# Describing the source of a contiguous load as 32 long rows while the destination keeps 128

## The chip, the cores and the metric

The kernel runs on one core of a Trainium2 chip. The metric is the device time of one launch in microseconds, the median of several executions. Besides the times there is one profiled execution, and all durations of single steps come from it.

## What is computed

The reference applies two layers to one token of width 640. Each layer is a sliding-window attention over a cache, followed by a mixer with an MLP, and both layers use the same weights and the same cache:

```python
x = x + _A_ref(_layernorm(x, axis=-1), A_k_cache, A_v_cache, A_wq, A_wo)
x = x + _B_ref(_layernorm(x, axis=-1), B_w1, B_w2, B_w3, B_w4)
x = x + _A_ref(_layernorm(x, axis=-1), A_k_cache, A_v_cache, A_wq, A_wo)
x = x + _B_ref(_layernorm(x, axis=-1), B_w1, B_w2, B_w3, B_w4)

def _A_ref(x, k_cache, v_cache, wq, wo):       # Hq = Hkv = 32, Dh = 192, Sk = 32768, D = 640
    W = min(4096, max(256, Sk // 4))           # 4096
    q = (x @ wq).reshape(B, Sq, Hq, Dh).transpose(0, 2, 1, 3)
    k = k_cache[:, :, Sk - W:, :]
    v = v_cache[:, :, Sk - W:, :]
    p = softmax(einsum("bhqd,bhkd->bhqk", q, k) * Dh ** -0.5)
    o = einsum("bhqk,bhkd->bhqd", p, v)
    return o.transpose(0, 2, 1, 3).reshape(B, Sq, Hq * Dh) @ wo

def _B_ref(x, w1, w2, w3, w4):                 # D = 640, F = 1536
    h = gelu(layernorm(x) @ w1)
    g0..g3 = quarters of h, shifted by one or two positions along S and padded with zeros
    x1 = x + concatenate([g0, g1, g2, g3]) @ w2
    return x1 + gelu(layernorm(x1) @ w3) @ w4
```

All tensors are bf16. As the sequence has one position, the shifted quarters are all zero, so w1 and w2 never matter and the kernel does not load them. Per layer and head it needs the last 4096 positions of K and V, 1.5 MiB each.

## The kernel before

One load of K or of V brings one head's window, 4096 x 192 values, into a buffer called a cell: 128 partitions with 6144 values (12,288 B) each, where partition p holds 32 consecutive positions. The source is contiguous through all partitions: the row of partition p + 1 starts in memory where that of p ends. There are twelve cells (`take` and `give` hand them out and take them back), shared by K, V, the transposed copies of K, the pieces of wo and the mixer's weights.

All loads are issued by SP on one queue, in the order of `stream`: wq in five pieces (`load_wq`, L178, one contiguous 128 x 6144 block each) with the input x after the first, then layer 0 and layer 1 by `layer_stream`. Within a layer the heads come in eight groups of four; a head's K load (`load_k`, L149) runs about a group ahead of its V load (`load_v`, L154), and after a group comes the piece of wo (`load_wo`, L182, 128 rows of 7,680 B, contiguous too) that its four heads need. A layer ends with w3 and w4 (`load_w3`, `load_w4`), whose rows are 2,560 and 3,072 B long. A few V loads are split into parts, each of which takes some columns of every row, and so do two pieces of wo at the end of layer 1. Layer 1 does not load K for heads 0 to 7 (`NKEEP`), since their transposed copies are kept, nor V of heads 2 and 3, and only a part of V for head 4.

SP issues a load as soon as its cell is free and the queue takes it. Per head, DVE transposes K in 32 x 32 blocks (L398), PE forms the scores (L474), the softmax follows for four heads at once (L494 to L561), PE multiplies with V (L590), DVE transposes the result (L597), and the group's output goes through wo. At the end of a layer the mixer (L881) multiplies with w3 (L922) and w4 (L969).

```python
    def load_k(layer, h):
        t = take(("k", layer, h))
        nc.sync.dma_start(t[:], A_k_cache[0, h, s0:Sk, :].rearrange("(p j) d -> p (j d)", p=P))
        return t
```

Of the kernel before, what the change touches and what calls it, by code (L numbers as in the profile page):

```python
# [2 lines left out]

# [14 lines left out]
P = 128  # L18
# [13 lines left out]
NJ4, NGK, NM = 4, 8, 4  # L32

RING = 1024


def shrink_ring(nc):


    nc.dynamic_dma_scratch_size = RING  # L40
    for a in nc.allocations:
        for m in getattr(a, "memorylocations", ()):
            if m.name == "DynamicDMAScratchLoc":
                m.dims = [P, RING]


@with_exitstack
def kernel(
# [13 lines left out]
):  # L62
    nc = tc.nc
    shrink_ring(nc)
    _, _, D = A_x.shape
    _, H, Sk, Dh = A_k_cache.shape
# [18 lines left out]
    s0 = Sk - W  # L85

    NA = Dh // 32
    NKX, NKL = 6, 8
    NKEEP, NCELL = 8, 12
# [11 lines left out]

    above, nc.sbuf_base = (nc.sbuf_base + 31) // 32 * 32, RING
    low = ctx.enter_context(tc.tile_pool(name="low", bufs=1))
# [18 lines left out]
        name=nc.get_next_instruction_name(), act_func_set_id=ACT_TABLE_SET, ins=[], outs=[]))  # L122

    wq_sb = fixed.tile([P, ND, HD], BF16, name="wq_sb")
# [10 lines left out]
    def take(key):  # L135
        i = free.popleft()
        cell_of[key] = i
        return (low if i == NCELL - 1 else cells).tile([P, FREE], BF16, tag=f"cell{i}", name=f"cell{i}")

    def give(key):  # L140
        free.append(cell_of.pop(key))

    def load_x():

        x_bf = wx_sb[0:ND, 4 * P:5 * P]
        nc.sync.dma_start(x_bf, A_x.rearrange("a b (n p) -> (a b n) p", p=P))
        return x_bf

    def load_k(layer, h):  # L149
        t = take(("k", layer, h))  # L150
        nc.sync.dma_start(t[:], A_k_cache[0, h, s0:Sk, :].rearrange("(p j) d -> p (j d)", p=P))
        return t

    def load_v(layer, h):  # L154
        t = take(("v", layer, h))
        src = A_v_cache[0, h, s0:Sk, :].rearrange("(p j) d -> p (j d)", p=P)
        cut = (2 * VW,) if h == VP else (FREE - VN, FREE - NKX * Dh) if h == VX else ()
        if h in GROUPS[layer][-1][-1 - layer:]:
            cut = FREE // 2,
        i = 0  # L160
        for e in cut + (FREE,):
            kept_v = h == VP or h == VX and i > 0
            if layer == 0 or not kept_v:
                nc.sync.dma_start(v_pair(t, h, i, e - i), src[:, i:e])
            i = e
        return t

    def v_pair(V, h, i, n):

        if h == VP and i >= 2 * VW:  # L170
            V, i = loaded["wo", 0, 0], i - 2 * VW + NA * D
        elif h == VX and i >= FREE - NKX * Dh:
            V, i = kx, i - (FREE - NKX * Dh)
        elif h == VX and i >= FREE - VN:
            V, i = kl, i - (FREE - VN)
        return V[:, i:i + n]

    def load_wq(layer, kc):  # L178
        nc.sync.dma_start(wq_sb[:, kc, :], A_wq[kc * P:(kc + 1) * P, :])
        return wq_sb  # L180

    def load_wo(layer, c):  # L182
        t = take(("wo", layer, c))
        src = A_wo[c * QC:(c + 1) * QC, :].rearrange("(p c) n -> p (c n)", c=NA)
        parts = {NG - 2: (3, 3), NG - 1: (3, 2, 1)}.get(c, (NA,)) if layer == 1 else (NA,)
        i = 0
        for n in parts:
            nc.sync.dma_start(t[:, i * D:(i + n) * D], src[:, i * D:(i + n) * D])
            i += n
        return t  # L190
# [13 lines left out]
    def load_w4(layer):  # L204
# [17 lines left out]
        return blocks  # L222

    LOADERS = {"x": load_x, "k": load_k, "v": load_v, "wq": load_wq, "wo": load_wo, "w3": load_w3, "w4": load_w4}

    def layer_stream(layer):
# [797 lines left out]
```

## Time and profile before

| | us |
|---|---|
| median of 3 runs | 515.57 (515.52 to 516.28) |
| the profiled execution, its own time | 515.88 |
| its span | 514.1 |
| PE busy | 325.7 (63%) |
| DVE busy | 291.2 (57%) |
| ACT busy | 48.9 (10%) |
| K load, 1536 KB, issue to landing (median) | 26.3 |
| V load, 1536 KB, issue to landing (median) | 27.3 |
| wo load, 960 KB, issue to landing (median) | 25.3 |

The span runs from the first to the last recorded instruction; the execution's own time has 1.8 us more around it. The granted TensorE clock was 0.669 on average. The loads read 214.5 MB. The line of slices cuts the span into 40 parts of 12.9 us, each digit a busy share in tenths; under it stands the rate at which data moved. In the view by windows the columns after the stretch are its length, the busy time of each engine with its instructions, the granted clock, the share of the 16 DMA engines' time that packets took, and the rate. In the chain of waits a line is start, length, and what the end of the program hung on then. Issue lines show the time at which SP handed a load over and how long the handing over took.

### The profile page before, as it was taken

The page shows a single profiled execution, that of the slowest core. Times are in us where ns is not written, and L with a number is a line of the kernel's source. Part 1 is how long each engine was busy: PE and PEld are TensorE (multiplying, and loading weights), DVE is VectorE, ACT ScalarE, POOL GpSimd, SP SyncE. Part 2 cuts the span into 40 slices and gives each one's busy share as a digit, 9 for nine tenths or more (in the row PEclk, how much of TensorE's full clock was granted, in tenths as well). Part 3 has the DMA queues.
Part 4 walks back from the last instruction along what each step waited for, and adds up shares of the span by engine and source line. Part 5 has one row for each costly group of instructions (what it writes and reads, how often), then busy time and mean ns, then how long its engine had stood idle before and what let it go on. Part 6 is the DMA issues. An engine that isn't in the chain of part 4 may idle for free.

```text
span 514.1 us, 9455 instructions
## 1 busy us (share of the span) xinstructions
PE 325.7 (63%) x4084; PEld 190.2 (37%) x4084; DVE 291.2 (57%) x587; ACT 48.9 (10%) x173; POOL 4.0 (1%) x16
## 2 busy tenths in 40 slices
PE   1057658656576645857655767667676766767665
PEld 0023334333333323534333544434343443335335
DVE  2077656676565755467623244666576566756722
ACT  1000101010010100101011111001010100100011
POOL 2000000000000000000000000000000000000000
PEclk9995777777665776576675585675565577656765
DMA  8999999999999999999999899999999999999996
GB/s 348 432 429 428 429 428 429 427 428 428 429 431 428 429 424 430 432 423 430 427 420 415 344 409 430 429 425 428 427 431 427 429 427 431 427 428 431 429 413 251
DMA packets 24093, 215.11 MB, mean 418 GB/s; under 512 B 2548, under 2 KB 3060, under 8 KB 9076
## 3 DMA queue, kind: packets, MB, share of 16 engines
q1 hardware_dynamic: 24052, 214.51, 99.0%
q8 instruction: 32, 0.52, 0.4%
q14 instruction: 9, 0.07, 0.0%
HBM read 214.50 MB, written 0.00 MB: 417 GB/s over the span
## 4 chain that ended last, share of the span: by engine, by line
DMA 54%; PE 23%; DVE 18%; issue 3%; ACT 1%; SPq 1%; DVEq 0%; ACTq 0%
DMA cell<-in_A_k_cache_dram 26%; DMA cell<-in_A_v_cache_dram 20%; DVE cell L398 13%; PE ST_ps L474 10%; PE O_ps L590 7%; DMA cell<-in_B_w_dram 4%; DMA cell<-in_A_wo_dram 4%; DVE o_sb L597 2%; PE qT_ps L428 1%; PE l_ps L549 1%; PE PT_ps L544 1%; PE nb_ps L522 1%; DVE pm L499 1%; DVE o_sb L533 1%; DVE V_ps L579 1%
## 5 line engine op out<-in xcount | busy, mean ns | idle before, releaser
L474 PE MATMUL ST_ps<-cell,Qblk 128*16 128x256 bf16 x1536 | 159.4, 375 | 104.9 <-DVE cell L398 68.4
L398 DVE STREAM_TRANSPOSE cell<-cell 128x768 uint32<-128x768 uint32 x224 | 200.4, 944 | 12.1 <-DMA cell<-in_A_k_cache_dram 11.8
L474 PEld LDWEIGHTS <-Qblk 128*16 128x16 bf16 x1536 | 83.7, 110 | 173.6 <-issue 147.5
L590 PE MATMUL O_ps<-cell,PT 128*2 128x384 bf16 x1010 | 101.3, 473 | 7.7 <-DMA cell<-in_A_v_cache_dram 5.6
L597 DVE STREAM_TRANSPOSE o_sb<-O_ps 128x384 f32<-128x384 f32 x64 | 37.2, 581 | 112.7 <-PE O_ps L590 112.6
L590 PEld LDWEIGHTS <-PT 128*2 128x2 bf16 x1024 | 46.2, 102 | 23.1 <-issue 14.6
L533 DVE STREAM_TRANSPOSE o_sb<-o_sb 128x256 bf16<-128x256 bf16 x16 | 7.1, 445 | 33.8 <-ACT o_sb L528 25.0
L605 ACT ACTIVATE oT<-oT_ps,rl 32x6 bf16<-32x6 f32 x40 | 10.3, 257 | 158.4 <-PE oT_ps L604 149.7
L604 PE MATMUL oT_ps<-o_sb,Lq 128*32 128x6 f32 x160 | 13.9, 195 | 11.1 <-DVE o_sb L597 10.6
L604 PEld LDWEIGHTS oT_ps<-o_sb,Lq 128*32 128x32 f32 x160 | 12.8, 144 | 21.6 <-issue 15.9
L610 ACT ACTIVATE oT<-oT_ps,rl 32x6 bf16<-32x6 f32 x24 | 6.2, 257 | 111.0 <-PE ST_ps L474 95.8
L428 PE MATMUL qT_ps<-xc,wq_sb 128*128 128x1 bf16 x210 | 7.2, 165 | 13.0 <-DMA wq_sb<-in_A_wq_dram 12.1
L417 PE MATMUL qr_ps<-wq_sb,xc 128*1 128x384 bf16 x90 | 14.1, 468 | 0.0
L442 DVE TENSOR_TENSOR Xq<-qT_ps,maskq 128x24 bf16<-128x24 f32 (+1 forms) x18 | 2.9, 162 | 18.2 <-PE qT_ps L428 17.5
L544 PE MATMUL PT_ps<-o_sb,Eq 128*32 128x32 bf16 x256 | 7.2, 237 | 9.2 <-DVE o_sb L533 4.0
L636 PE MATMUL yr_ps<-cell,oT 128*1 128x320 bf16 x108 | 12.3, 380 | 0.0
L428 PEld LDWEIGHTS <-wq_sb 128*128 128x128 bf16 x210 | 6.8, 104 | 14.2 <-DMA wq_sb<-in_A_wq_dram 13.2
L525 ACT COPY nb_sb<-nb_ps 128x1 f32<-128x1 f32 x16 | 2.6, 160 | 94.4 <-PE nb_ps L522 94.4
L549 PE MATMUL l_ps<-lh,ones 128*128 128x4 f32 x32 | 8.4, 334 | 4.9 <-ACT PT L547 4.9
L544 PEld LDWEIGHTS <-Eq 128*32 128x32 bf16 x256 | 5.5, 111 | 16.0 <-issue 15.9
L609 PE MATMUL oT_ps<-o,Lq 128*32 128x6 f32 x48 | 6.1, 200 | 6.0 <-DVE o L608 6.0
L522 PEld LDWEIGHTS nb_ps<-ones,o_sb 1*128 1x128 f32 x32 | 7.1, 275 | 7.2 <-issue 5.4
(146 smaller groups left out, 196.8 us busy)
## 6 DMA issues: line engine op xcount, KB each, us to landing
cell<-in_A_k_cache_dram SPq DMA_DIRECT2D x56, 1536.0 KB, 26.3
cell<-in_A_v_cache_dram SPq DMA_DIRECT2D x56, 1536.0 KB, 27.3
cell<-in_A_wo_dram SPq DMA_DIRECT2D x13, 960.0 KB, 25.3
wq_sb<-in_A_wq_dram SPq DMA_DIRECT2D x5, 1536.0 KB, 12.2
cell<-in_A_v_cache_dram SPq DMA_DIRECT2D x6, 768.0 KB, 23.3
cell<-in_A_v_cache_dram SPq DMA_DIRECT2D x2, 864.0 KB, 9.0
cell<-in_B_w_dram SPq DMA_DIRECT2D x1, 1536.0 KB, 12.0
cell<-in_B_w_dram SPq DMA_DIRECT2D x2, 768.0 KB, 10.3
```

Source lines behind the costliest of these rows:

```text
L398: nc.vector.transpose(Tu, Ku[:, :, q * NY:(q + 1) * NY])
L417: nc.tensor.matmul(qr_ps[32 * i:32 * i + 1, :], lhsT=xc[:, kc:kc + 1], rhs=wq_sb[:, kc, t0 * P + i * N:t0 * P + (i + 1) * N], start=(kc == ...
L428: nc.tensor.matmul(qT_ps[:, tl:tl + 1], lhsT=wq_sb[:, kc, t * P:(t + 1) * P], rhs=xc[:, kc:kc + 1], start=(kc == 0), stop=(kc == ND - 1))
L474: nc.tensor.matmul(ST_ps[r:r + QW, :].rearrange("p (g i) -> p g i", g=ng), lhsT=Q[:, n, :], rhs=T4[:, :, f, :, t], start=(hq == 0 and n == ...
L522: nc.tensor.matmul(nb_ps[:], lhsT=held["w"], rhs=ones[0:1, 0:1], start=True, stop=True)
L533: nc.vector.transpose(held["PrT"], held["Pr"])
L544: nc.tensor.matmul(PT_ps[32 * m:32 * (m + 1), :, :, ng * q:ng * (q + 1)], lhsT=Eq[:, q, :], rhs=src[:, m:QW:NM], start=True, stop=True)
L549: nc.tensor.matmul(l_ps[:], lhsT=ones[:], rhs=held["lh"][:], start=True, stop=True)
L590: nc.tensor.matmul(O_ps[r:r + 2, :], lhsT=PT[:, hq, 2 * i:2 * i + 2], rhs=v_pair(V, h, 2 * i * Dh, 2 * Dh), start=(i < 4), stop=(i >= NB - 4))
L597: nc.vector.transpose(o_sb[:], O_ps.rearrange("p (e a c) -> p e c a", e=2, c=NA))
L604: nc.tensor.matmul(oT_ps[r, :], lhsT=Lq[:], rhs=o_sb[:, e, :, e], start=(e == 0), stop=(e == 1))
L636: nc.tensor.matmul(yr_ps[32 * i:32 * i + 1, :], lhsT=oT[:, k:k + 1], rhs=wo_t[:, k * D + i * N:k * D + (i + 1) * N], start=(k == 0), stop= ...
```

## The change

A helper `load_wide` issues a load whose source is described as 32 rows, each four times as long, and whose destination is described as before. The instruction is put together by hand, since the two sides have different shapes; both name the same bytes in the same order, and it goes to the same queue on SP. `load` chooses between it and `dma_start`. All K loads use it except the first K load of layer 1; all V loads that aren't split, except heads 0 and 1 in layer 1; wq except its first piece; wo where it is not split. The order of the loads and all other instructions stay.

```diff
+WIDE = 4
...
+def load_wide(nc, dst, src):
+    wide = src.rearrange("(g w) n -> g (w n)", w=WIDE)
+    assert [list(d) for d in wide.ap] == [[WIDE * src.shape[1], P // WIDE], [1, WIDE * src.shape[1]]]
+    sym = [mybir.BassSymbolicTensorAccessPattern(ap=a.ap, dtype=a.dtype, bass_ap=a) for a in (wide, dst)]
+    return nc.sync.add_instruction(mybir.InstDMACopy(
+        name=nc.get_next_instruction_name(), ins=sym[:1], outs=sym[1:], queue="qSPDynamicHW", mode="Copy"))
...
+    def load(dst, src, wide=True):
+        (partial(load_wide, nc) if wide else nc.sync.dma_start)(dst, src)
...
     def load_k(layer, h):
         t = take(("k", layer, h))
-        nc.sync.dma_start(t[:], A_k_cache[0, h, s0:Sk, :].rearrange("(p j) d -> p (j d)", p=P))
+        load(t[:], A_k_cache[0, h, s0:Sk, :].rearrange("(p j) d -> p (j d)", p=P), (layer, h) != (1, NKEEP))
...
     def load_v(layer, h):
...
-            if layer == 0 or not kept_v:
+            if not cut:
+                load(t[:], src, layer == 0 or h >= 2)
+            elif layer == 0 or not kept_v:
                 nc.sync.dma_start(v_pair(t, h, i, e - i), src[:, i:e])
...
     def load_wq(layer, kc):
-        nc.sync.dma_start(wq_sb[:, kc, :], A_wq[kc * P:(kc + 1) * P, :])
+        load(wq_sb[:, kc, :], A_wq[kc * P:(kc + 1) * P, :], kc > 0)
...
     def load_wo(layer, c):
...
+        if len(parts) == 1:
+            load(t[:, 0:NA * D], src)
+            return t
         for n in parts:
             nc.sync.dma_start(t[:, i * D:(i + n) * D], src[:, i * D:(i + n) * D])
```

More of the change, by code (lines that the diff above doesn't have):

```diff
@@ L2 @@
 from contextlib import ExitStack
+from functools import partial
 import concourse.bass as bass
```

## The prediction

> **What bounds the kernel now.** I read the page's slices first, because they say whether any engine is busy all the time. None of the compute engines is; the DMA engines are.
>
> ```profile
> span 514.1 us, 9455 instructions
> PE 325.7 (63%) x4084; PEld 190.2 (37%) x4084; DVE 291.2 (57%) x587; ACT 48.9 (10%) x173; POOL 4.0 (1%) x16
> ...
> DMA  8999999999999999999999899999999999999996
> GB/s 348 432 429 428 429 428 429 427 428 428 429 431 428 429 424 430 432 423 430 427 420 415 344 409 430 429 425 428 427 431 427 429 427 431 427 428 431 429 413 251
> DMA packets 24093, 215.11 MB, mean 418 GB/s; under 512 B 2548, under 2 KB 3060, under 8 KB 9076
> ...
> q1 hardware_dynamic: 24052, 214.51, 99.0%
> ```
>
> PE works 63% of the span and DVE 57%, while the DMA engines stand at nine tenths or more in nearly all 40 slices, at 423 to 432 GB/s in the steady ones. The loads' queue, q1, fills 99.0% of 16 engines' time. The only visible hole is the slice of 344 GB/s, near 289 us, where the first layer's mixer hands over to the second layer's attention.
>
> Next the stretches, from the view by windows, and the queue's issues in order of time:
>
> ```profile
> core 0: us, PE busy (x) PEld busy (x) DVE busy (x) ACT busy (x) POOL busy (x), PEclk, DMA share, GB/s
> 108.26:139.84 31.58, 19.93 (x219) 11.06 (x218) 19.75 (x37) 3.04 (x10) 0.00 (x0) 0.72 1.01 428
> ...
> 340.00:380.00 40.00, 29.13 (x314) 15.57 (x309) 25.00 (x47) 5.28 (x17) 0.00 (x0) 0.56 1.01 428
> ...
> 276.00:284.00 8.00, 5.25 (x118) 4.17 (x110) 2.11 (x16) 1.64 (x8) 0.00 (x0) 0.50 1.00 397
> ...
> 288.00:292.00 4.00, 3.48 (x76) 2.35 (x79) 0.90 (x6) 0.30 (x2) 0.00 (x0) 0.50 0.81 308
> ...
> 111.96 0.33 SPq L164 DMA_DIRECT2D cell<-in_A_v_cache_dram  x1
> 115.61 0.33 SPq L151 DMA_DIRECT2D cell<-in_A_k_cache_dram  x1
> 119.25 0.33 SPq L164 DMA_DIRECT2D cell<-in_A_v_cache_dram  x1
> ```
>
> A DMA share of 1.01 means that no engine rests and that neighbouring packets overlap a little. SP hands over a load every 3.65 us, and its own issue takes 0.33 us. A group of four heads (eight K or V loads and one wo load) repeats every 31.58 us. Where rows are shorter (276 to 284 us, the mixer's weights, rows of 2,560 and 3,072 B) the same full share moves only 397 GB/s: rows cost something beyond their bytes.
>
> Last the chain of waits, to see whether the compute side would keep up if the loads came faster:
>
> ```profile
> 76.72 27.84 DMA cell<-in_A_k_cache_dram
> ...
> 108.26 27.84 DMA cell<-in_A_k_cache_dram
> ...
> 423.61 28.41 DMA cell<-in_A_v_cache_dram
> 452.09 28.39 DMA cell<-in_A_v_cache_dram
> ...
> 499.91 10.49 DMA cell<-in_B_w_dram
> ```
>
> The chain is nearly all DMA up to 200 us and again from 423.6 to 510.4 us. A load takes about 28 us from issue to landing: 7.6 loads of 3.65 us stand in line, so what a load waits for is its turn. From 285 to 423 us the chain runs through PE and DVE steps. It is the time in which compute, left behind at the layers' border, catches up, while the queue stays full.
>
> **What one row costs.** The trace records each packet: rows of 12,288 B take 460 ns (median of 14,976), 7,680 B 291, 3,072 B 121, 1,280 B 55, and the 4 B that report a landing 9 ns. From 55 to 460 ns that is (460 − 55)/(12,288 − 1,280) = 0.03679 ns per byte, and 460 − 452.1 = 7.9 ns per row that no byte explains; 291 and 121 ns fit the same line. But packets overlap, so the wall pays less. One engine moves (8 × 1,572,864 + 983,040)/16 = 847,872 B in a group; at 0.03679 ns per byte this is 31.19 us of the 31.58. The remaining 386 ns are spread over 72 rows and 9 reports: 4.8 ns each. So 7.9 ns is the upper price of a row on the wall, 4.8 ns what the queue in motion shows.
>
> **The change, part by part.** It removes no byte and no load, and it leaves the order on every engine alone. What it changes is the source side of 126 loads: 55 of K, 54 of V, 4 of wq, 13 of wo. Each reads 32 rows of 49,152 B (30,720 B for wo) instead of 128; the destination keeps its 128 rows. Per engine a wide load reads 2 rows, not 8, so 126 × 6 = 756 source rows per engine go away. Left as they were: the first wq load, the second layer's first K load and first two V loads, all split loads, the mixer's weights.
>
> The cost of a source row by itself is not shown: in all rows of this trace source and destination have equal lengths. It is bounded by 0 (the destination's rows carry the whole cost) and 7.9 ns; below 0 is possible if unequal sides lose the overlap (a rival below). I take 4.8 ns, all of it on the source side, since that is what the full queue shows in the very stretches where the wide loads lie. 756 × 4.8 ns = 3.6 us. By 7.9 ns it would be 6.0 us, by 0 nothing.
>
> [...]
>
> All of the saving lies on the path, as the wide loads lie in stretches with a share of 1.01. In the hole about 1.4 us of DMA time is lost because cells are not free (shares of 0.81, 0.92 and 0.96 in three windows of 4 us from 288 us on, against 1.01); it starts from the landing of the first layer's w4, comes earlier with it, and stays. The tail from 510.4 us stays as well. Between 285 and 423 us compute covers its lag: its groups there take 29.6 and 30.3 us (same DVE step at 349.38, 379.02 and 409.31 us) against the queue's 31.58. With a group of loads at 31.58 − 54 × 0.0048 = 31.32 us it still gains 1.0 to 1.7 us per group, where it gained 1.3 to 1.9. The lag it made up by 423 us, in 4.5 groups, is some 7 us; at the new rate that takes about five groups, to 445 us, well before the loads end. If that cover were gone, the second layer's share of the gain (53 of the 126 loads, 1.5 us) would go with it.
>
> SP's instruction has sides of unequal shape now. Its price isn't in the trace. Nearest rows: 0.33 us for an even load, 0.38 to 0.50 us for the mixer's three-dimensional ones. Anything below 3.65 us is hidden behind the queue in motion; at the start, four wq loads take 2.19 us to issue, and a rise to 0.5 us each adds nothing, as the queue has a load to move by then. I price it at 0, with up to 0.5 us if the start shows it.
>
> Sum: the profiled execution took 515.88 us (span 514.1, 1.8 around it), 0.31 over the median of 515.57. 515.88 − 3.6 = 512.3 on its own scale, and 512.0 on the median's. A kernel of this spread can tell 0.2%, 1.0 us, from no change.
>
> **The rivals.**
>
> Destination rows set the pace. Each engine still writes 128/16 = 8 rows of 12,288 B per load, and if the 4.8 ns belong to writing, or the generator cuts the long row to the shorter side, nothing moves: 515.6. For it: the price of a row is known only with both sides together. Against it: nothing in the trace. 0.12.
>
> The memory sets the pace, whatever the rows. Then too 515.6. Against it speaks the window of 397 GB/s with short rows at full share beside 428 with long ones. [...] 0.02.
>
> Slower: unequal sides lose the overlap. Today each packet overlaps the next by 7.9 − 4.8 = 3.1 ns. If with one read feeding four writes every destination row pays its full 7.9 ns, 126 × 8 = 1,008 rows per engine pay 3.1 ns more: +3.1 us, 518.7. A pause between long reads decides: there are 252 per engine, so the 3.6 us are used up at 14 ns per long read, and beyond that the kernel is slower. For it: no row in the trace has unequal sides, so a pause of that size is not excluded. Against it: the report of 4 B between rows costs only 9 ns. 0.18.
>
> A part of the gain: both sides share the cost, or the start of layer two gives some back. 513 to 514.5, counted with faster.
>
> [...]
>
> **How the numbers follow.** The forecast with its spread, from a part of the gain to 7.9 ns per row (509.6 to 514.5), has 0.68; no change 0.14; slower 0.18. The range runs from 509.3, the upper price, to 516.2, which takes in no change and its scatter; outside it lie most of the slower case and a few hundredths below. The likeliest case alone spans 509.6 to 514.5.
>
> **What would show it.** Right: q1 falls from 24,052 packets by up to 126 × 96 = 12,096, the steady slices rise from 428 to 431 or 433 GB/s, a group repeats in 31.3 us, the first layer's w4 lands near 283 instead of 285.1 us, and the hole keeps its depth. Wrong in size: the count falls and the slices stay at 428 (destination rows pay). Wrong in sign: the slices fall below 427, or the share of the steady windows drops under 1.00, which would be pauses between long reads. If the slices rise but the end does not come earlier, the chain from 285 us on must show compute to the end.

## The result: 0.23% faster, a third of the forecast

The changed kernel's median is 514.79 us and that of the kernel before 515.86 us, 17 runs of each in turns; the ratio is 0.9977, 95% interval 0.9969 to 0.9986, that is 1.2 us less (0.7 to 1.6). The forecast was 3.6 us less. The profiled execution took 513.87 us with a span of 512.1. It is the quickest of the 17, while the profiled execution of the kernel before, 515.88 us, lies at its median; so the 2.0 us between the two traces' spans flatter the change.

The page of the changed kernel:

```profile
span 512.1 us, 9455 instructions
...
DMA  8999999999999999999999999999999999999996
GB/s 369 430 430 427 432 439 430 439 427 415 454 433 427 434 408 425 430 416 451 428 403 417 351 444 427 424 436 420 434 427 420 430 439 427 424 439 430 419 407 240
DMA packets 11997, 215.11 MB, mean 420 GB/s; under 512 B 2548, under 2 KB 3060, under 8 KB 7412
...
q1 hardware_dynamic: 11956, 214.51, 98.4%
```

q1 has exactly the 12,096 packets fewer that the long rows allow: the trace has 3,616 packets of 49,152 B, 1,820 ns each in the median, where a packet of 12,288 B took 460. The queue's packet time sank from 99.0% of 514.1 us to 98.4% of 512.1, by 5 us per engine. The steady slices now jump between 408 and 454 GB/s, because the page books a packet as a whole where it begins and a packet is four times as large; only long windows can be compared. Two of them, the view by windows of the kernel before:

```profile
core 0: us, PE busy (x) PEld busy (x) DVE busy (x) ACT busy (x) POOL busy (x), PEclk, DMA share, GB/s
20.00:260.00 240.00, 151.33 (x1723) 85.78 (x1723) 149.74 (x262) 19.81 (x68) 0.00 (x0) 0.70 1.01 428
310.00:470.00 160.00, 110.02 (x1243) 61.29 (x1235) 102.81 (x181) 15.83 (x54) 0.71 (x2) 0.60 1.01 428
```

and of the changed kernel:

```profile
20.00:260.00 240.00, 152.15 (x1725) 87.12 (x1726) 149.61 (x262) 20.20 (x70) 0.00 (x0) 0.73 1.00 430
310.00:470.00 160.00, 110.14 (x1236) 61.97 (x1236) 102.43 (x181) 15.60 (x53) 0.71 (x2) 0.61 1.00 431
```

The rate rose in both, but the share fell from 1.01 to 1.00. Some 2 of the 5 us reached the wall, as the next sums show; the rest, by the share, was time in which packets had overlapped.

To compare finer than this view, I spread every loading packet's bytes evenly over its own time. From 20 to 260 us the rate, which I call the steady rate, is then 427.2 GB/s before and 429.3 after, +0.5%. From the same sums comes the time at which so many bytes had moved. Against the kernel before, the changed one gains 1.15 us between 10 and 110 MB (the first layer's stream) and 0.84 us between 130 and 210 MB (the second's), 2.0 us together. I call this sum the stream's gain; it leaves out the start, the border of the layers and the end. About 115 of the 126 wide loads lie in those bytes, so it is 17.3 ns per load.

SP's issues, in order of time, show the other difference, 0.47 us each instead of 0.33:

```profile
111.23 0.47 SPq L55 DMA_DIRECT2D cell<-in_A_v_cache_dram  x1
115.05 0.47 SPq L55 DMA_DIRECT2D cell<-in_A_k_cache_dram  x1
118.67 0.47 SPq L55 DMA_DIRECT2D cell<-in_A_v_cache_dram  x1
```

### The profile page after: what moved, and what is told of

Same layout as the page of the kernel before. It is cut to its first block, busy times and chain, and to the rows that moved or that the text cites. A ratio compares the mean times of both kernels' runs of the same rounds, so it can differ in the third digit from the quotient of the medians.

```text
span 512.1 us, 9455 instructions
## 1 busy us (share of the span) xinstructions
PE 326.1 (64%) x4084; PEld 191.4 (37%) x4084; DVE 290.9 (57%) x587; ACT 48.8 (10%) x173; POOL 4.0 (1%) x16
## 3 DMA queue, kind: packets, MB, share of 16 engines
q1 hardware_dynamic: 11956, 214.51, 98.4%
## 5 line engine op out<-in xcount | busy, mean ns | idle before, releaser
L494 PE MATMUL ST_ps<-cell,Qblk 128*16 128x256 bf16 x1536 | 161.3, 378 | 102.7 <-DVE cell L418 67.9
```

Of the source, the lines that this page charges most:

```text
L494: nc.tensor.matmul(ST_ps[r:r + QW, :].rearrange("p (g i) -> p g i", g=ng), lhsT=Q[:, n, :], rhs=T4[:, :, f, :, t], start=(hq == 0 and n == ...
```

## The experiments

**A stream of loads alone.** Two questions: what does a row cost on either side, and does the kernel's other work eat part of the gain? The first kernel holds nothing but loads, described in several ways:

```diff
+        for rs, rd in SEGMENTS:          # rows of the source and of the destination
+            for _ in range(LOADS):
+                load(nc, t[:], src, rs, rd)
```

> Leaves the whole computation out: it only streams K loads of 1.5 MiB into ten buffers, 20 loads per stretch, and writes zeros. Eight stretches, told by source rows / destination rows of a load per DMA engine: 8/8 as before, 2/8 as in the change, 4/8, 16/16, 8/16, 4/16, then 8/8 and 2/8 again. In the profiled runs of the two kernels the steady rate from 20 to 260 us was 427.2 and 429.3 GB/s, that is 7.0 ns per row over the bytes before, and 2.9 ns saved per source row taken away. Theory A (both sides pay: a source row 2.9 ns, a destination row 4.1 ns): 427.4, 429.5, 428.8, 421, 423.6, 425 GB/s in order. Rival B (a source row costs all of the 7.0 ns, but a long read that feeds several destination rows pauses about 12 ns): 427.4, 429.3, 424.8, 421, and 416 or less for 8/16. Rival C (all cost on the source side and no pause; what is missing in the kernel is lost to the kernel's own traffic): 427.4, 432.5, 430.8, 421, 427.4, 431.

Measured from the packets in the middle of each stretch: 8/8 427.2, 2/8 426.4, 4/8 426.3, 16/16 417.6, 8/16 417.8, 4/16 417.8, then 426.3 and 426.4 GB/s. None of the theories said this. Apart from the first stretch, whose 427.2 comes from its first loads (below), the number of source rows means nothing here; only the destination's count does, by (3,765 − 3,689)/8 = 9.5 ns per row. Yet the kernel had gained. A difference between the two was the address: these buffers began 128 B past a multiple of 256 B in their partition, the kernel's cells at multiples of 256. So I streamed again with both.

> Leaves the whole computation out, as the first stream did, with 16 loads per stretch. In that one the buffers began 128 B past a multiple of 256 B in each partition; the kernel's cells begin at multiples of 256. Here six stretches begin at multiples of 256 (source rows / destination rows per load and engine: 8/8, 2/8, 4/8, 16/16, 8/16, 4/16), then 128 B past it 8/8 and 2/8, 64 B past it 8/8, and 128 B past it 8/16. Theory M (an engine reads and writes side by side, and the slower side sets the pace; 8.1 ns per source row, about 5 ns per destination row that begins at a multiple of 256 B, 9 ns for one that does not): 427, 429.5 to 430, the same for 4/8, 420, 426, 426, then 426.3, 426.3, about 426.3, and 417.8 GB/s. Theory S (costs of both sides add up, 2.9 and 1.1 ns in the kernel, and the stream alone differed because no other engine touched the memory): addresses change nothing, so 8/8, 2/8 and 4/8 stand at 426 to 427 and all stretches with 16 destination rows at 417.7.

| source/destination rows per engine and load | destination row begins at a multiple of 256 B plus | GB/s, mean of the stretch | ns per load |
|---|---|---|---|
| 8/8 | 0 | 430.0 | 3,657 |
| 4/8 | 0 | 431.8 | 3,642 |
| 2/8 | 0 | 432.6 | 3,636 |
| 8/16 | 0 | 429.2 | 3,664 |
| 4/16 | 0 | 429.7 | 3,661 |
| 16/16 | 0 | 425.7 | 3,695 |
| 8/8 | 128 | 426.4 | 3,688 |
| 2/8 | 128 | 426.4 | 3,689 |
| 8/8 | 64 | 426.2 | 3,690 |
| 8/16 | 128 | 417.8 | 3,765 |

The view by windows of this stream shows the stretches with 12,288-byte packets (8/8 and 8/16 on a multiple of 256 B, and in the other order of addresses 8/8 and 8/16 at 128 B past):

```profile
core 0: us, DVE busy (x) POOL busy (x), PEclk, DMA share, GB/s
10.00:53.00 43.00, 0.00 (x0) 0.00 (x0) 1.00 1.01 430
245.00:287.00 42.00, 0.00 (x0) 0.00 (x0) 1.00 1.01 429
362.00:405.00 43.00, 0.00 (x0) 0.00 (x0) 1.00 1.01 427
539.00:583.00 44.00, 0.00 (x0) 0.00 (x0) 1.00 1.01 417
```

With the source held at 8 rows, twice the destination rows cost 0.8 GB/s in the first pair and 8.6 in the second, by the table. On multiples of 256 B the two sides seem to add up: a source row costs (3,657 − 3,636)/6 = 3.6 ns, and from 8/16 to 16/16 it is 3.8; a destination row costs 0.9 ns beside 8 source rows. 128 B past them, eight more destination rows cost 77 ns (3,688 and 3,765), 9.6 ns each, and the source's rows nothing (3,688 with 8, 3,689 with 2). Theory M expected the role of the address, but by its prices it said 420 for 16/16; theory S had the sums and missed the address. So I took theory A2 into the next runs: costs add up while destination rows are aligned; otherwise the destination's rows alone set the pace.

Two things speak against adding up. In the table four source rows are worth 3 ns from 8/16 to 4/16, not 14; and the first stream's first stretch was faster than its repeat. Taken load by load, from the same packets, the stretches show why:

| stretch | ns of its loads, in order |
|---|---|
| 8/8 on a multiple of 256 B | after the first load, 3,657 or 3,658 each to the end |
| 2/8 on a multiple of 256 B | six of 3,629 or 3,630, one of 3,633, then 3,640 each to the end |
| 8/16 on a multiple of 256 B | 3,658 or 3,659 for most of the first eight (one 3,698), 3,662, then 3,665 or 3,666 |
| 8/8 at 128 B past, first in its stream | after the first load four of 3,657 or 3,658, 3,675, then 3,688 to 3,690 |

The last three begin at a pace that goes by their source rows (3,658 ns for 8 rows, whatever the destination; 3,630 for 2) and settle at a slower one. 4/16, which follows 8/16, has no fast loads at its start (3,661 ns in the mean). What goes on inside an engine no trace shows, so I take these times for a model: each side of a load has a time of its own, the first loads of these three show the source's, and in a settled stretch the longer of the two is the pace. Read so, the source side takes 3,630 ns with 2 rows, 3,658 with 8 and 3,695 with 16, that is 4.6 to 4.7 ns per source row. The destination side takes 3,640 ns with 8 aligned rows and 3,661 to 3,666 with 16, and off the multiples 3,689 and 3,765. The slower side sets the pace; this gives every settled stretch of the second stream within 5 ns. It is theory M with other prices. I fitted these prices to the traces, and no run was made to test them on new shapes, 1 source row for instance; the kernels below are the check that there is.

**The form of the instruction alone.** `WIDE = 1` keeps the hand-made instruction and describes 128 source rows:

```diff
-WIDE = 4
+WIDE = 1
```

> The changed kernel's 126 loads with the hand-made instruction, but described as 128 source rows again, so that only the form of the instruction differs from the kernel before. Theory A and rival B: the form costs SP's queue 0.47 instead of 0.33 us per load, hidden behind the queue in motion, at most 0.4 us at the start: ratio 1.000 to 1.001. Rival D (the form gives part of the gain back, which is why 2.2 us from the rate became 1.1 us in the median): about +1 us, ratio 1.002.

Ratio 1.0012 (0.9999 to 1.0025): the interval takes in no change, and the median alone does not refute rival D. The trace does: steady rate 427.2 GB/s, stream's gain 0.02 us, issues at 0.47 us. The first 10 MB arrived 0.22 us later than in the first trace of the kernel before, but so they did in a second trace of that kernel (below). The form costs SP time that nobody waits for, as far as the traces can tell. Where this trace lost 1.0 us is the border of the layers, to which I come back.

**Half the widening.** `WIDE = 2`.

> The source described as 64 rows of twice the length: 4 instead of 6 source rows per load and engine go away, 504 in all. Theory A: two thirds of the change's gain, 1.5 us by the rate, ratio about 0.9975 to 0.9985. Rival B: twice as many pauses of 12 ns, -20 ns per load and engine times 126: 2.5 us slower than before, ratio 1.005. Rival C: 504 rows of 7.0 ns, 3.5 us, less what the kernel loses.

Ratio 0.9978 (0.9965 to 0.9992), stream's gain 1.76 us, 429.0 GB/s. Rival B, a pause for each long read, falls: twice as many long reads should have made it slower than before. Theory A's two thirds are too little as well; from 8 to 4 rows brings 1.76 of the 2.0 us, the next halving the rest. That is what the slower side gives: settled, the stream's 4/8 takes 3,642 ns and its 2/8 3,640, 16 and 18 ns under the 3,658 of 8/8, and 115 loads make 1.8 and 2.1 us of it. Had the two sides added up at 3.6 ns per source row, six rows would have brought 2.5 us. This answers the second question as well: the kernel's 17.3 ns per load are all but the 18 ns of the bare stream, so the kernel's other work eats hardly any of the gain.

**More rows on the destination, and on both sides.** The two edits in `load_wide`:

```diff
+    rows = src.rearrange("(g w) n -> g w n", w=WIDE)          # 128 source rows
+    halves = dst.rearrange("p (a n) -> p a n", a=2)           # 256 destination rows
...
+    halves = [a.rearrange("p (a n) -> p a n", a=2) for a in (src, dst)]   # 256 rows on both
```

> The same 126 loads with the source rows of the kernel before (128) and the destination described as 256 rows of half the length (6,144 B; 3,840 B for wo): 8 more destination rows per load and engine, 1,008 in all. Theory A: 1,008 x 4.1 ns = +4.1 us, ratio 1.008, packets in the trace possibly unchanged in number. Rival B: every read now feeds two rows and pauses: 1,008 x 12 ns = +12 us, ratio 1.023. Rival C (the destination's rows cost nothing): ratio 1.000.

> The 126 loads of the change with 256 rows of half the length on both sides: 8 more source rows and 8 more destination rows per load and engine than the kernel before. With 256 destination rows alone it was 1.0027. Theory M: the source side sets the pace, 8 x 8.1 = 65 ns per load and engine, 126 loads: +8.2 us, and about 0.4 us at the start from the form of the instruction: ratio 1.016 to 1.017. Theory S: 8 x (2.9 + 1.1) = 32 ns per load: +4.0 us and the start: ratio 1.0085.

The first gave 1.0027 (1.0015 to 1.004) and a stream's gain of −0.97 us: with some 920 added rows in those bytes (115 loads, 8 rows each) 1.1 ns per destination row, not the 4.1 of theory A, and not rival C's nothing. Per load it is 8.4 ns; settled, the stream's 8/16 lies 8 ns above its 8/8. The second gave 1.0085 (1.007 to 1.01) and −4.31 us, 37.5 ns per load; the stream's 16/16 lies 37 ns above 8/8. That is theory S's ratio (to the last digit by chance, as the interval shows). It refutes the 8.1 ns that theory M had for a source row, but not its slower side: at the 4.7 ns by which the first loads of 2/8 undercut 8/8, eight more source rows make 37 ns on the source side alone. The second one's steady windows:

```profile
20.00:260.00 240.00, 149.24 (x1698) 85.57 (x1698) 148.76 (x259) 19.38 (x66) 0.00 (x0) 0.72 1.02 424
310.00:470.00 160.00, 104.57 (x1261) 60.26 (x1263) 100.63 (x177) 15.89 (x54) 0.71 (x2) 0.69 1.02 424
```

424 GB/s at a share of 1.02: nothing here shows an engine at rest, and the edit added nothing but rows. SP now needs about 3.4 us to hand over a load of K or V, but such a load still lands some 24 us after its issue, so about six stand in line and SP isn't what they wait for.

**The cells moved by 128 B**, in both kernels, to see whether the address matters outside a bare stream:

```diff
-    above, nc.sbuf_base = (nc.sbuf_base + 31) // 32 * 32, RING
+    above, nc.sbuf_base = (nc.sbuf_base + 31) // 32 * 32, RING + 128
...
-    head = ctx.enter_context(tc.tile_pool(name="head", bufs=1))
     fixed = ctx.enter_context(tc.tile_pool(name="fixed", bufs=1))
     cells = ctx.enter_context(tc.tile_pool(name="cells", bufs=1))
+    head = ctx.enter_context(tc.tile_pool(name="head", bufs=1))
```

`RING + 128` moves one of the cells; wq and the other cells move because the pool `head`, 128 B per partition, no longer lies ahead of them.

> The kernel before with all cells and wq moved by 128 B in each partition, so that no destination row begins at a multiple of 256 B; nothing else changes. Theory A2 (source rows 3.7 ns and destination rows some 1 ns add up as long as destination rows begin at multiples of 256 B; otherwise the writing side alone sets the pace, 3,689 ns per load whatever the source): by the stream, 3,688.5 - 3,657.5 = 31 ns per load of 1.5 MiB, 136 such loads' worth of bytes: +4.2 us, ratio 1.008. Rival (the address matters only in a bare stream): ratio 1.000.

> The changed kernel with the same move by 128 B. Theory A2: the long source rows bring nothing any more; as slow as the kernel before with the move, ratio about 1.008, the steady rate equal in both. Rival: the gain stays, ratio 0.997 to that of e9's.

1.0105 (1.0089 to 1.0121) and 1.0097 (1.0083 to 1.0112): moved, both are slower by some 5 us, and nothing is left of the change that these runs can tell. It is more than the 1.008 expected, as the start, the border and the end (5.4 and 5.1 us late by 214 MB) lost something as well. The first layer's window of the moved kernel before:

```profile
20.00:260.00 240.00, 152.92 (x1698) 86.13 (x1698) 149.01 (x259) 19.43 (x66) 0.00 (x0) 0.67 1.01 424
```

and of the moved changed kernel:

```profile
20.00:260.00 240.00, 152.34 (x1703) 86.89 (x1704) 149.13 (x259) 19.68 (x67) 0.00 (x0) 0.68 1.00 424
```

By packets it is 423.2 and 423.3 GB/s, and the stream's gains are −3.87 and −3.84 us, equal whatever the source rows, as A2 and the slower side both have it. The share differs (1.01 and 1.00) while the rate doesn't: with the cells moved, overlapping packets bring nothing that the traces can tell.

**The start, and the change again.** One kernel left wq and the first five K loads as they were; the other is the changed kernel once more.

> The changed kernel with wq and the first five K loads left as they were before (9 of the 126 loads), so that the first loads are issued in 0.33 us each again. If the form of the instruction delays the start, the 0.25 to 0.45 us by which the first issues came later go, and 9 x 18 ns = 0.16 us of the gain are lost: 0.1 to 0.3 us better than the change, ratio about 0.997. If the start costs nothing: 0.16 us worse. The issue times of the first ten loads in the trace tell these apart, the median hardly.

> The changed kernel once more, with these runs of the kernel before, and a second trace of it. By the steady rate (429.3 against 427.2 GB/s, 0.5% of some 480 us) less the later start it should be 1.9 us faster, ratio 0.9963; by the runs so far 0.9977. If the trace again shows 429.3 GB/s and a span about 2 us shorter, what is missing in the median comes from runs that differ elsewhere, at the border of the layers.

Ratios 0.9963 (0.9949 to 0.9978) and 0.9965 (0.9950 to 0.9980), not to be told apart. With the loads at the start as before, SP's first issues do come up to 0.5 us earlier, and the first 10 MB arrive no earlier (26.1 us, against 25.8 to 26.0 in three traces of the change): the start was not worth repairing, and I have no version that beats the change. The second trace of the change has 429.3 GB/s and a stream's gain of 2.02 us again, but a span of 514.4 us. Between 118 and 130 MB, at the border, it fell back by 1.2 us. So the border had to be looked at with traces of both kernels.

> A second trace of the kernel before. So far the two traces with a granted clock of 0.86 to 0.90 from 290 to 302 us lost nothing more at the layers' border, and those with 0.51 to 0.67 lost 1.1 to 1.4 us there, in kernels of either kind. If the clock there is chance, the kernel before shows both values too, with a loss of 1 us or more of transfer progress between 118 and 130 MB when it is low.

> A third trace of the changed kernel. The steady rate should stand at 429.3 GB/s from 20 to 260 us again, and the transfers' progress should gain some 1.1 us on the kernel before from 10 to 110 MB and 0.9 us from 130 to 210 MB; between them the border decides, by its clock, whether the end comes 0.7 or 2.3 us earlier.

From 290 to 302 us, the kernel before a second time, the kernel with `WIDE = 1`, the change again, and its third trace, in this order:

```profile
290.00:302.00 12.00, 9.74 (x227) 6.33 (x227) 3.78 (x10) 0.47 (x2) 0.00 (x0) 0.83 0.93 349
```

```profile
290.00:302.00 12.00, 11.65 (x218) 7.14 (x222) 3.09 (x8) 0.46 (x2) 0.00 (x0) 0.51 0.93 353
```

```profile
290.00:302.00 12.00, 10.34 (x212) 6.89 (x213) 4.06 (x11) 0.53 (x3) 0.00 (x0) 0.67 1.07 404
```

```profile
290.00:302.00 12.00, 8.95 (x234) 6.51 (x227) 4.11 (x12) 1.28 (x5) 0.00 (x0) 0.92 1.06 417
```

The column before the share is the granted clock: 0.83, 0.51, 0.67, 0.92. PE is busy for 8.95 to 11.65 of these 12 us, and cells become free as it gets on: from 288 to 303 us SP waits 11.0 us for PE's scores in the first trace of the kernel before and 9.9 us in that of the change. The five traces with 0.83 or more lost at most 0.4 us between 118 and 130 MB against the first trace, and three of them gained; of the five below 0.7, four lost 0.7 to 1.2 us and one 0.4; two between, 0.72 and 0.76, lost 0.1 or nothing. These figures include the streams' own rates: at 423 GB/s the 12 MB take 0.25 us longer anyway, so the kernel before with moved cells, the one that lost 0.4, lost less than 0.2 at the border, at a clock of 0.51. The clock alone doesn't settle it. Both clocks occur with the long source rows, and low ones also with 128 source rows (`WIDE = 1`, and the kernel before with moved cells), so the long rows are not needed for the low clock. The kernel before itself showed the high one in both its traces, so the half of my expectation that it would show both was not met. That a low clock costs the microsecond is argued from these traces and not shown; I had no means to set it.

## Why the prediction was right in kind and wrong in size

The mechanism holds in kind: the packets go by the source's rows while the destination keeps its 128 (24,052 with 128 source rows, also beside 256 destination rows, and 11,956 with 32), the queue stays full but for the border (a share of 1.00 in both long windows), and the count fell as forecast. The start and SP's longer issue cost nothing that the traces can tell, as priced. The first layer's w4 landed at 284.0 us, half of the way from 285.1 to the 283 that was named as a sign.

The step that failed is the sum 756 × 4.8 ns, with "all of it on the source side": it lets all six source rows of a load count in full. The source side does gain about that much: with six rows fewer the first loads of the aligned stream's 2/8 took 3,630 ns and not 3,658, 28 ns or 4.7 per row. But after seven of them the stream settled at 3,640 ns, in the model the time of eight destination rows, and only 18 ns lie between this and the 3,658 of the loads before. So 126 loads are worth 18 × 126 = 2.3 us, not 3.6, and the kernel's stream shows 2.0 us in 115 of them. Per removed row that is 2.9 ns on average: 3.8 for the first four of a load (`WIDE = 2`, 1.76 us over 460 rows) and 1.0 for the last two. The prediction had the writing side only as an all-or-nothing rival and not as a floor within the sum. It did list "A part of the gain", but as both sides sharing the cost.

That 4.8 ns is near the price of a source row is luck. The 31.58 us between two issues was taken for the time of a group's transfers; by the steady rate that group of 13.57 MB takes 31.76 us, and this excess over the bytes is 563 ns, not 386. The same division would then have given 7.0 ns per row and 5.3 us. Part of that excess belongs to the reports (nine in a group, 9 ns each) and to the queue that the page lists as instruction (0.4% of the engines' time). The change took 159 ns of the 563 out of a group, again 2.9 ns for each of its 54 rows. The range's lower end, 509.3, is called the upper price, which gives 509.6.

Of the 2.3 us that the 126 loads are worth the comparison of times shows 1.2 (0.7 to 1.6) in the first series and 1.8 (1.0 to 2.6) in the repeat. The traces' ends came earlier by 2.3, 2.4 and 0.7 us, and their difference is the border, where "the hole keeps its depth" was too simple: the progress from 118 to 130 MB differs by 1.6 us between traces of the same changed kernel. The tail wasn't quite fixed either: after 214 MB it lasts 6.0 to 7.3 us in the traces of both kernels. How often the hole is deep in each kernel was not measured, so whether the remaining microsecond of the first series is that alone stays open.

The rivals: "destination rows set the pace" was given 0.12 for a gain of nothing. It fails in that form, but it is the floor that cut the sum, and with cells 128 B further on it is what the runs show in full (stream's gains of −3.87 and −3.84 us); nothing in the prediction looked at addresses. "Unequal sides lose the overlap" named something real, since the share fell from 1.01 to 1.00, and put its cost too high: the rate rose where the overlap went (427.2 to 429.3 GB/s), and `WIDE = 2` refuted a pause of the size supposed. The share itself was a poor sign: with the moved cells it fell from 1.01 to 1.00 in the same way, and the rate stayed. The memory as the limit falls too: the kernel's 427.2 GB/s became 429.3, and the aligned stream reached 432.6.

## What to carry to other kernels

Where loads run without a gap, try a price for each side of a load and let the slower one set the pace. Here the model that fitted has 4.6 to 4.7 ns per source row, against a floor of 3,640 ns for eight aligned destination rows of 12,288 B. Describing contiguous sources as longer rows brought 0.2 to 0.35% here, and rows of twice the length already brought nearly nine tenths of the stream's gain. First look where destination rows begin: 128 B past multiples of 256 B the same kernels took 1% longer, and longer source rows brought nothing that could be told. And beside the median, measure a change in a saturated queue by the transfers' progress between fixed amounts of bytes, since the end carries the chance of everything else, here 1.6 us at the layers' border alone.

## What was not expected of the hardware

A destination row that begins 64 or 128 B past a multiple of 256 B costs the bare stream some 4 ns more, 3,657 against 3,688 to 3,690 ns per load of eight rows. 64 and 128 B cost the same within 2 ns per load: 3,690 and 3,688.

The cost of a bad address shows late: in the first stream four loads after the first still ran at 3,657 or 3,658 ns before the pace fell to 3,689. A short test would have missed it.

A sum of packet times can fall by more than the gain: q1's packets took 5 us less per engine, and 2 us of it reached the wall.
